# A stored shift for each attention step, applied to the list scheduler's order

## The chip, the cores and the metric

One core of one Trainium2 chip. The metric is device time in microseconds (us) of one execution. The engines are TensorE (PE; its weight loads are PEld), VectorE (DVE), ScalarE (ACT), GpSimd (POOL) and SyncE (SP, which issues most transfers). Each has its own instruction stream.

## The reference

Attention with heads mixed before and after the softmax (4 batches, 12 heads, 448 rows, 64 columns), then a SoLU layer with a layer norm (1792 tokens, 768 to 1024 to 768).

```python
scores = scale * np.matmul(q, k.transpose(0, 1, 3, 2))
scores = np.einsum('bhij,hg->bgij', scores, w_pre)
attn = softmax(scores)                       # max, exp, sum
attn = np.einsum('bhij,hg->bgij', attn, w_post)
x = np.matmul(attn, v)                       # -> (B*S, H*D)
...
h = x @ w_in
solu = h * softmax(h)
ln = (solu - mu) / np.sqrt(var + 1e-06) * g_ln
out = ln @ w_out
```

## The kernel before

Two stages run one after the other, each written as tasks (`add`, key first) that a list scheduler, `Plan.order`, puts into one list. The list is then walked and each task emits its instructions. So what the list sets is the order of the instructions within each engine's stream and nothing else: two neighbours of the list on different engines start when their inputs are there. An engine works its own stream in that order, and an instruction that waits holds up all that stands behind it on that engine.

The attention has 2629 tasks. A batch has four blocks of rows (three of 120 rows, one of 88); a block is cut into units of ten rows, taken in pairs. The tasks of a pair and their lines:

- `qk` (PE, L559): scores of two heads into two PSUM banks; `sh` (ACT, L571) writes the float16 upper half, `sl` (DVE, L576) the remainder and frees the bank. Six `qk` fill a block.
- `f` (SP): a transfer that brings ten rows of all heads together. `m` (PE, L629): the mix over heads, one step for a pair of units.
- `mx` (DVE, L639): row maximum of a unit; `ex` (ACT, L655): its exponentials and their sum; `gd`, `iv` (DVE, L666 and L670): guard and reciprocal for the pair; `w` (POOL, L676): the second mix's weights divided by the sum; `o` (PE, L684): the second mix, transposed; `po` (ACT, L284): its copy out of PSUM, which frees one of two banks.
- `av` (PE, L733): times v, six steps a block; `xh` (ACT), `xl` (DVE): the result as two float16 halves.

Beside it run tasks of the next batch: loads `ld`, maxima `am`, scale chains `sc` (one small PE step each, L247, tile `spread_...`), and the split of q and k, `hi` (POOL, L277) and `lo` (DVE L280, or POOL L473 and L474). In the last batch the input weights of the second stage are converted (`wi`), measured (`wm`) and split (`wh`, `wl`), and the first tile's `h0` products (PE, L905) are slipped in. `warm` tasks are small PE products without a use for the result; `ident` (POOL) makes the identity that they and the `tp` steps at the start need.

The order comes from `Plan.order`: at each turn, the engine that can start earliest takes, among what is ready within a short look ahead, the task with the lowest due time. Due times are written by hand and moved for each kind by `AIM`; costs are fixed numbers for each task; `LAG` adds to the landing time of a kind's transfers; `TURN` is a charge where PE changes between kinds of product; `behind` makes one task stand after another in the list.

```python
for _, e, _, run in plan.order():
    run(e)
```

The second stage (`moe`, its own plan) multiplies tile after tile by the input weights (PE, L905), normalises on DVE, ACT and POOL, and multiplies by the output weights (PE, L1528).

Of the kernel before, what the change touches and what calls it, by code (L numbers as in the profile page):

```python
# [18 lines left out]
class Plan:  # L19
# [15 lines left out]
    }  # L35
    LAG = {
        "fw": 10, "ld": 4.24, "t": 3, "xd": 7.9,
    }

    def __init__(self, **rings):  # L40
        self.size = rings
# [31 lines left out]
    def order(self):  # L73
        done, out = {}, []
# [31 lines left out]
        while len(out) < len(tasks):  # L106
            best = None
            for e, t0 in free.items():
# [21 lines left out]
            _, _, e, k, t = best  # L130
            run, on, _, _, ring, slots, dma = tasks[k][:7]
# [19 lines left out]
                    avail.add(n)  # L151
            out.append((t, e, k, run))
        return out


@with_exitstack
def kernel(
# [45 lines left out]
    NXG = NPAIR // XG  # L203
# [111 lines left out]
    plan = Plan(raw=2, hl=2, v=NV, S=2, s=2, sr=AHEAD, m=3, o=2, e=NE, w=NWR, p=RING, x=1, X=1)  # L315
# [598 lines left out]
    def add_tasks():  # L914
# [49 lines left out]
        for b in range(B):  # L964
# [4 lines left out]
            for n in "kq":  # L969
# [4 lines left out]
                for i in range(pieces):  # L974
# [5 lines left out]
                        behind=[("ld", n, b, i - 1)] if i else [("ld", "k", 0, pieces - 1)] if z and n == "q" else [],  # L980
# [145 lines left out]
            for u in range(NU):  # L1126
# [85 lines left out]
            for blk in range(NBLK[b]):  # L1212
# [18 lines left out]
                for g in range(NXG):  # L1231
                    due = av_at[XG * g + XG - 1] + 1.1
                    add(
                        ("xh", b, blk, g),
                        one(x_hi, b, blk, g),
                        {"act": (0.45, 0.57)},
                        after=[("av", b, blk, XG * (g + 1) - 1)] + ready,
                        due=due,
                        ring="X" if blk == g == 0 else None,
                        until=[("xd", b, i) for i in range(XP)],  # L1240
                    )
                    add(
                        ("xl", b, blk, g),
                        one(x_lo, b, blk, g),
                        {"dve": (0.75, 0.84)},
                        after=[("xh", b, blk, g)],
                        due=due + 0.7,
                    )
# [71 lines left out]
    with tc.manual_schedule():  # L1320
# [11 lines left out]
        add("clear", lambda e: [nc.vector.memset(t, 0.0) for t in ams.values()], {"dve": 0.5}, due=-1.0)  # L1332
        nc.vector.memset(bias64, -8.0 * (1023 - 127 + 20) * 2.0**20)
        add_tasks()
        for _, e, _, run in plan.order():
            run(e)
        st.close()

# [383 lines left out]
```

## Time and profile before

| | us |
|---|---|
| median of three runs (687.9 to 694.23) | 691.94 |
| the profiled execution | 690.71 |
| its span, first to last instruction | 689.0 |
| PE busy | 643.7 |
| DVE busy | 498.0 |
| ACT busy | 455.3 |
| POOL busy | 276.7 |

The attention's PE work ends a little after 460 us, where that of the second stage follows at once. A row of the timeline gives the start, the length, the engine and line, what it writes and reads, how many instructions are merged, and in brackets the idle time before them and what ended it. The ends of PE's products are modelled and run past the start of the next; so the time that PE spends on a step is read here from its start to the start of the next one. PEclk is the granted clock as a share of full speed (2.4 GHz); 0.50 is 1.2 GHz.

### The profile page before, as it was taken

The numbers are of one execution on the slowest core, as the hardware profiler recorded it, in microseconds if no ns is written. First come the engines' busy times: TensorE is split into PE (matmuls) and PEld (weight loads), VectorE is DVE, ScalarE is ACT, GpSimd is POOL, SyncE is SP. The second block draws the span as 40 slices with busy tenths as digits, with TensorE's granted clock in tenths as the row PEclk, the third lists the DMA queues.
The fourth block names the chain that finished last, engine by engine and source line by source line (L and its number), as shares of the span: only waits on it lengthen the run. The fifth ranks groups of instructions, "written<-read, shape, count | busy, mean of one in ns | idle before, by whom it ended". The sixth has DMA issues, their size and how long they took to land. (4 is left out here: it accounts for less than half of the span.)

```text
span 689.0 us, 17773 instructions
## 1 busy us (share of the span) xinstructions
PE 643.7 (93%) x6660; PEld 431.5 (63%) x6660; DVE 498.0 (72%) x1322; ACT 455.3 (66%) x989; POOL 276.7 (40%) x427
## 2 busy tenths in 40 slices
PE   6878999999889999899899988899999989999997
PEld 6545667777666777667677666775444435666664
DVE  5978997789978689987879999946888998200000
ACT  3867978998779988887888987552456666411111
POOL 2223871247741337851214323611667746410000
PEclk9989999999999999999989999999999999999999
DMA  9157458467777566978336843107956532451121
GB/s 237 29 146 228 158 134 190 158 181 205 214 143 143 130 191 189 244 197 235 128 113 209 272 147 95 27 2 218 225 145 142 104 61 54 89 126 46 47 64 52
DMA packets 114030, 98.54 MB, mean 143 GB/s; under 512 B 69604, under 2 KB 104600, under 8 KB 113944
## 3 DMA queue, kind: packets, MB, share of 16 engines
q1 hardware_dynamic: 108120, 83.62, 45.9%
q0 software_dynamic: 4416, 12.40, 6.5%
q10 hardware_dynamic: 1408, 1.38, 0.7%
q8 instruction: 53, 0.87, 0.5%
q14 instruction: 33, 0.27, 0.1%
HBM read 33.24 MB, written 9.63 MB: 62 GB/s over the span
## 5 line engine op out<-in xcount | busy, mean ns | idle before, releaser
L684 PE MATMUL po<-wr,e 128*112 128x120 f32 x1440 | 184.1, 278 | 14.1 <-POOL wr L676 12.2
L684 PEld LDWEIGHTS po<-wr,e 128*112 128x112 f32 x1440 | 161.3, 181 | 53.4 <-POOL wr L676 27.4
L676 POOL TENSOR_SCALAR wr<-wq,sm 128x120 f32<-128x120 f32 x180 | 69.2, 393 | 211.0 <-DVE sm L670 117.4
L655 ACT ACTIVATE e<-pm,nb,c_exp 128x448 f32<-128x448 f32 x180 | 131.7, 733 | 26.3 <-DVE dead L639 24.0
L639 DVE TENSOR_SCALAR_CACHE_REDUCE dead<-pm,c_nexp 128x448 f16<-128x448 f32 x180 | 121.6, 676 | 15.9 <-PE pm L629 9.2
L284 ACT COPY p_t<-po 112x480 f32<-112x480 f32 x180 | 109.5, 618 | 28.3 <-PE po L684 26.9
L576 DVE SCALAR_TENSOR_TENSOR s<-ps,s 120x448 f16<-120x448 f32 (+1 forms) x192 | 112.3, 616 | 16.3 <-ACT s L571 15.2
L571 ACT ACTIVATE s<-ps 120x448 f16<-120x448 f32 (+1 forms) x192 | 93.8, 545 | 18.9 <-PE ps L559 16.9
L733 PE MATMUL px<-p_t,raw_v 112*64 112x120 f32 (+3 forms) x1632 | 88.0, 259 | 2.0 <-ACT e L655 0.8
L905 PE MATMUL ps_h<-wi,xf 128*128 128x512 f16 x396 | 86.1, 379 | 2.6 <-DVE u L1455 2.6
L559 PE MATMUL ps<-k,q 64*64 64x448 f16 (+2 forms) x1008 | 81.8, 362 | 6.5 <-DVE s L576 5.1
L733 PEld LDWEIGHTS px<-p_t,raw_v 112*64 112x64 f32 x1632 | 76.0, 137 | 15.3 <-issue 9.1
L1528 PE MATMUL y<-wo_h,lth 128*128 128x384 f16 (+2 forms) x224 | 73.0, 326 | 0.0
L1528 PE MATMUL y<-wo_l,lth 128*128 128x384 f16 (+2 forms) x224 | 73.0, 326 | 0.0
L1528 PE MATMUL y<-wo_h,ltl 128*128 128x384 f16 (+2 forms) x224 | 73.0, 326 | 0.0
L905 PEld LDWEIGHTS <-xf 128*128 128x128 f16 x396 | 38.7, 98 | 49.3 <-issue 3.1
L1540 ACT ACTIVATE o<-y,c_out 128x384 f32<-128x384 f32 (+2 forms) x28 | 16.2, 579 | 72.6 <-PE y L1528 72.6
L629 PE MATMUL pm<-sr,wp_hi 64*64 64x448 f16 x720 | 59.1, 366 | 5.2 <-DMA sr<-s 3.2
L1528 PEld LDWEIGHTS <-lth 128*128 128x128 f16 x448 | 43.8, 98 | 29.3
L559 PEld LDWEIGHTS <-q 64*64 64x64 f16 (+2 forms) x1008 | 32.8, 107 | 33.6 <-issue 16.2
L1513 POOL TENSOR_TENSOR ll<-u,lh 128x1024 f16<-128x1024 f32 x14 | 31.6, 2258 | 16.7 <-ACT lh L1509 10.8
L666 DVE TENSOR_SCALAR sm<-sm 128x2 f32<-128x2 f32 (+1 forms) x92 | 25.2, 275 | 17.7 <-ACT e L655 16.9
(182 smaller groups left out, 823.4 us busy)
## 6 DMA issues: line engine op xcount, KB each, us to landing
sr<-s SPq DMA_DIRECT2D x176, 210.0 KB
cv_wi<-in_moe_w_in_dram SPq DMA_DIRECT2D x24, 256.0 KB
cv_wo<-in_moe_w_out_dram SPq DMA_DIRECT2D x8, 768.0 KB
raw_k<-in_k_dram POOLq DMA_DIRECT2D x18, 224.0 KB, 4.3
raw_q<-in_q_dram POOLq DMA_DIRECT2D x18, 224.0 KB, 6.2
raw_v<-in_v_dram POOLq DMA_DIRECT2D x18, 224.0 KB, 4.8
xh<-xsh SPq DMA_DIRECT2D x9, 224.0 KB
xl<-xsl SPq DMA_DIRECT2D x9, 224.0 KB
```

The lines of the kernel that those rows point to most:

```text
L284: nc.scalar.copy(out=out, in_=in_)
L559: nc.tensor.matmul(sps[b, c, h + e][lo:hi], q2[b, g][rows, 2 * j + x, i0 + lo : i0 + hi], k1[b, g][rows, 2 * j + y], start=(a == 0), stop= ...
L571: nc.scalar.activation(out=s_t[b, c][0 : y.shape[0], h, 0], in_=y, func=AF.Copy, scale=2.0**-E_S)
L576: nc.vector.scalar_tensor_tensor(out=t[:, h, 1], in0=y, scalar=2.0**-E_S, in1=t[:, h, 0], op0=ALU.mult, op1=ALU.subtract)
L629: nc.tensor.matmul(pmx[b, u + i][64 * e : 64 * e + 64, 0:S], w[rows], sr[b, u][rows, e, z], start=(a == 0), stop=(a == 2),)
L639: nc.vector.tensor_scalar(out=dead, in0=pmx[b, u][:, 0:S], scalar1=c_nexp[0:UK, b : b + 1], scalar2=None, op0=ALU.mult, op1=ALU.min, accum ...
L655: nc.scalar.activation(out=ee[b, u], in_=pmx.pop((b, u))[:, 0:S], func=AF.Exp, bias=nbs.pop((b, u)), scale=c_exp[0:UK, b : b + 1], accum_o ...
L676: ENG[eng].tensor_scalar(out=w, in0=wq[0:UK, 0 : H * UN], scalar1=sm, scalar2=1.0, op0=ALU.mult, op1=ALU.mult)
L684: nc.tensor.matmul(ps[:, c * 120 : (c + 1) * 120], e[:, c * CP : (c + 1) * CP], w, start=True, stop=True)
L733: nc.tensor.matmul(xps[b, blk, g][e * 64 : e * 64 + 64, i, cut], raws["v", b, p][:, e, c * D : (c + 1) * D], next(x for y, x in block_view ...
L905: nc.tensor.matmul(ps[:, n], xx[:, kc, o : o + 128], ww[:, kc, n * 512 : (n + 1) * 512], start=(kc == 0 and a == 0), stop=(kc == KDM - 1 a ...
L1528: nc.tensor.matmul(ys[t, n], lts[t, x][:, kc], w[:, kc, c0:c1], start=(kc == 0 and a == 0), stop=(kc == KFF - 1 and a == 2),)
```

## The change

`Plan` gets a list of 2629 whole numbers, `SHIFT`, and a function that applies it: the task at place i of the new list is the one that stood at place i plus the i-th number. Three inputs of the scheduler change too: `LAG` has 1 us more for the transfers `f`; the second `ex` of a pair stands behind the first in the scheduler's list; and `xh` steps stand behind each other in order. The tasks themselves, their buffers, the engines they run on and the second stage's plan are as they were.

```diff
     LAG = {
-        "fw": 10, "ld": 4.24, "t": 3, "xd": 7.9,
+        "f": 1, "fw": 10, "ld": 4.24, "t": 3, "xd": 7.9,
     }
+
+    SHIFT = """
+    2 2 3 3 3 3 6 7 1 -8 0x2 -12 -9 15 20 16 20 21 21 88 7 -4 1 113 102 32 30 -15 -3 75 17 -9 -13 -13 15
+    -9 16 22 -14 -25 14 23 68 -28 17 63 111 -18 -18 -16 -10 -16 -15 -12 -12 -12 -11 -11 -10 -27 -16 -10
...
+    1 1 1 1 1 2 -51 -1 0x11
+    """
...
+    def shifted(self, out):
+
+        moves = []
+        for x in self.SHIFT.split():
+            a, _, n = x.partition("x")
+            moves += [int(a)] * int(n or 1)
+        return [out[i + a] for i, a in enumerate(moves)]
...
                     one(expo, *g),
                     {"act": (0.701, 0.816)},
                     after=[("mx",) + g],
+                    behind=[("ex", b, u0)] if u != u0 else [],
...
                         one(x_hi, b, blk, g),
                         {"act": (0.45, 0.57)},
                         after=[("av", b, blk, XG * (g + 1) - 1)] + ready,
+                        behind=[("xh", b, blk, g - 1)] if g else [("xh", b, blk - 1, NXG - 1)] if blk else [],
...
-        for _, e, _, run in plan.order():
+        for _, e, _, run in plan.shifted(plan.order()):
             run(e)
```

## Rows read from the trace of the kernel before

**Rows 1.** Busy time by stretch: stretch, its length, engines, clock, DMA share, GB/s
```profile
60.00:460.00 400.00, 376.56 (x4760) 280.19 (x4760) 345.60 (x953) 330.05 (x763) 183.12 (x331) 0.98 0.60 165
460.00:560.00 100.00, 96.93 (x615) 46.74 (x614) 81.31 (x173) 48.98 (x77) 55.00 (x35) 1.00 0.61 149
560.00:689.00 129.00, 124.78 (x744) 72.61 (x742) 26.54 (x69) 37.26 (x59) 23.29 (x16) 1.00 0.28 68
```
**Rows 2.** PE's timeline in a stretch without gaps
```profile
130.66 0.57 PE L629 MATMUL pm<-sr,wp_hi 64*64 64x448 f16 x8
...
131.25 0.74 PE L559 MATMUL ps<-k,q 64*64 64x448 f16 x12
131.92 1.07 PE L684 MATMUL po<-wr,e 128*112 128x120 f32 x8
132.93 1.04 PE L733 MATMUL px<-p_t,raw_v 112*64 112x120 f32 x16
...
136.13 1.90 PE L684 MATMUL po<-wr,e 128*112 128x120 f32 x16
137.95 0.76 PE L559 MATMUL ps<-k,q 64*64 64x448 f16 x12
...
142.78 0.57 PE L629 MATMUL pm<-sr,wp_hi 64*64 64x448 f16 x8
...
143.47 1.07 PE L684 MATMUL po<-wr,e 128*112 128x120 f32 x8
```
**Rows 3.** Groups by line, 60 to 440 us: busy us, mean ns, idle before, releasers
```profile
L684 PE MATMUL po<-wr,e 128*112 128x120 f32 x1327 | 168.8, 277 | 10.9 <-POOL wr L676 9.1 <-ACT p_t L284 1.1 <-issue 0.2
...
L655 ACT ACTIVATE e<-pm,nb,c_exp 128x448 f32<-128x448 f32 x165 | 120.8, 733 | 22.4 <-DVE dead L639 20.2 <-DVE sm L666 1.6
...
L284 ACT COPY p_t<-po 112x480 f32<-112x480 f32 x166 | 101.0, 619 | 21.2 <-PE po L684 19.7
...
L277 POOL TENSOR_SCALAR hl_q<-raw_q,p_q 112x512 f16<-112x512 f32 x18 | 13.3, 760 | 0.9 <-DVE p_q L232 0.7
```
**Rows 4.** PE's timeline, four of its nine longest gaps, first and last among them
```profile
183.15 1.89 PE L684 MATMUL po<-wr,e 128*112 128x120 f32 x16 [1.58 <-POOL wr L676]
...
285.69 3.45 PE L684 MATMUL po<-wr,e 128*112 128x120 f32 x16 [2.19 <-POOL wr L676]
...
342.18 0.75 PE L559 MATMUL ps<-k,q 64*64 64x448 f16 x10 [1.47 <-DVE s L576]
...
446.11 3.45 PE L684 MATMUL po<-wr,e 128*112 128x120 f32 x16 [2.01 <-POOL wr L676]
```
**Rows 5.** DVE's timeline ahead of the last of these gaps
```profile
439.16 6.05 DVE L280 SCALAR_TENSOR_TENSOR wi<-wi,p_wi,wi 128x1024 f16<-128x1024 f32 x3
445.14 0.16 DVE L666 TENSOR_SCALAR sm<-sm 128x2 f32<-128x2 f32 x1
```
**Rows 6.** ACT's timeline ahead of the first of these gaps
```profile
178.50 0.72 ACT L655 ACTIVATE e<-pm,nb,c_exp 128x448 f32<-128x448 f32 x1
...
179.21 0.61 ACT L284 COPY p_t<-po 112x480 f32<-112x480 f32 x1
179.69 0.74 ACT L655 ACTIVATE e<-pm,nb,c_exp 128x448 f32<-128x448 f32 x1
```
**Rows 7.** Busy time at half clock, three of four stretches, first and last among them, as rows 1
```profile
41.00:46.00 5.00, 4.24 (x44) 1.70 (x35) 3.71 (x11) 2.62 (x7) 0.78 (x3) 0.50 0.53 139
...
344.00:350.00 6.00, 6.00 (x40) 3.92 (x32) 4.42 (x11) 3.81 (x9) 0.00 (x0) 0.50 0.48 163
446.00:449.00 3.00, 2.89 (x14) 2.89 (x15) 3.00 (x4) 0.61 (x1) 0.40 (x2) 0.50 0.00 0
```
**Rows 8.** PE's timeline, its first products
```profile
5.77 3.38 PE L539 MATMUL warm<-ident 128*128 128x128 f16 x30 [5.77 <-POOL ident masks.py:199]
```
**Rows 9.** Line 280 on DVE: durations in ns (least, median, most), first and last start
```profile
L280 DVE SCALAR_TENSOR_TENSOR hl_k<-raw_k,p_k,hl_k x20: 466/724/909, 90.7 to 289.3; 112x256 f16<-112x256 f32 x20
L280 DVE SCALAR_TENSOR_TENSOR hl_q<-raw_q,p_q,hl_q x18: 467/480/946, 96.3 to 299.2; 112x256 f16<-112x256 f32 x18
```

More of the change, by code (lines that the diff above doesn't have):

```diff
@@ L36 @@
     LAG = {
-        "fw": 10, "ld": 4.24, "t": 3, "xd": 7.9,
+        "f": 1, "fw": 10, "ld": 4.24, "t": 3, "xd": 7.9,
     }
+    SHIFT = """
+    2 2 3 3 3 3 6 7 1 -8 0x2 -12 -9 15 20 16 20 21 21 88 7 -4 1 113 102 32 30 -15 -3 75 17 -9 -13 -13 15
+    -9 16 22 -14 -25 14 23 68 -28 17 63 111 -18 -18 -16 -10 -16 -15 -12 -12 -12 -11 -11 -10 -27 -16 -10
+    -7 0 3 4 -8 -5 2 5 7 0 -12 -20 -9 -2 0 1 2 -13 -8 -13 0x4 2 -1 -9 0 1 -16 -11 1 6 -8 -4 0 11 -9 2 4
[8 rows of a table added]
+    1 8 0 2 -4 -2 4 -1 5 -15 -11 -7 -4 18 -3 -3 0 4 -3 0 -3 -1 4 0 3 8 4 -3 -6 -4 -2 1 6 -4 0x4 1 -25
@@ new lines @@
+    0x2 2 -1 4 0 5 8 5 9 4 -1 -6 -1 6 6 16 0 4 6 -17 -14 5 1 -8 -2 4 4 7 10 -4 6 -4 9 4 -2 7 3 -29 5 -4
+    4 10 4 -3 1 12 13 1 2 3 -3 3 8 14 2 6 7 1 16 5 24 4 0 3 -11 4 7 9 14 8 9 7 -4 8 16 -5 15 -5 8 9 5 8
+    16 -8 -4 15 10 14 15 4 15 1 3 13 22 14 11 14 14 0 8 21 12 20 25 13 11 12 18 4 10 13 16 24 21 0 14 10
+    -35 -32 -26 -17 -94 -90 -75 -107 -71 -30 -57 -27 1 -6 0x2 4 -1 5 -1 9 5 -1 4 14 8 17 1 -4 3 4 -9 4
+    -8 -3 5 -6 4 -1 7 2 8 5 5 8 5 7 7 -4 7 11 7 -1 12 5 12 13 3 5 14 17 3 4 -71 6 6 -63 -32 -23 -30 -15
@@ new lines @@
+    -14 -10 2 -6 1 6 -5 -4 10 11 0 -2 9 2 2 8 8 -4 -4 10 12 1 4 -15 3 -13 -7 -20 0 1 -5 3 -1 2 5 10 -3
+    0x2 -3 0 3 8 8 3 -3 -5 2 -2 -1 -7 1 1 1 1 2 0 1 3 0 2 -1 2 2 4 4 0x2 2 -6 3 0 3 -1 2 -1 1 -60 1 1 3
+    3 -4 5 5 7 0 3 -3 4 6 0 -5 4 1 -1 -14 1 3 0 3 -1 0 2 2 2 5 9 4 5 -6 -3 -3 2 6 -5 -3 1 1 9 1 1 7 1 1
+    2 5 -4 4 8 -4 3 3 -3 8 9 0 4 0 4 -23 -2 -61 -3 -11 5 0x2 4 -4 4 -2 7 4 7 -4 8 5 -3 -3 -2 4 -9 6 2 6
+    -18 1 -8 1 2 2 2 3 -11 0 2 2 2 6 9 -4 -1 -16 2 2 2 5 -6 -6 1 2 -8 -3 1 7 0 2 -4 2 8 -4 -4 -3 -1 1 5
@@ new lines @@
+    7 -3 3 3 4 8 -4 -10 -8 3 -1 -8 -2 -2 0x3 2 2 8 1 5 9 10 4 -2 9 -10 -10 20 2 3 4 6 7 -11 1 -8 -13 -17
[12 rows of a table added]
+    4 -3 0 2 -1 2 2 2 -2 1 -10 2 2 -1 2 -4 -1 1 2 0 4 1 3 0 5 1 2 9 13 -2 -13 1 3 -12 -3 -1 13 0x3 -7 1
+    -12 2 6 14 1 4 5 11 -10 3 4 -7 -11 8 1 -13 3 8 -8 -3 0 -15 2 3 4 -12 -4 3 7 -6 -3 8 -1 0 11 -1 1 11
+    -9 10 -8 5 1 -5 7 15 1 3 -6 7 -14 7 2 9 -14 -14 8 -5 -5 -4 -3 -17 -3 2 2 -4 -3 0 6 0 -2 0 16 0 6 -5
+    -4 -2 13 -2 1 13 -4 0x2 1 -4 8 -3 3 3 -2 -5 7 11 21 7 -21 -19 -2 1 -2 8 4 -6 -3 3 -17 -4 -3 3 11 -1
[13 rows of a table added]
@@ new lines @@
+    -54 -40 -37 -30 -26 -7 -2 -20 -19 30 1 7 1 -12 0x2 -4 -1 27 2 3 -4 -3 -1 2 -5 -2 17 0 18 0 3 0 3 3
+    -8 -11 1 18 11 13 -8 -2 0 -9 4 6 -1 7 5 8 13 8 15 18 6 3 5 7 -17 9 9 -221 3 9 12 -72 -57 -27 -21 -19
+    -14 -5 -2 0 1 -13 -2 1 4 7 7 -4 6 0x2 5 11 8 8 35 -9 8 -7 7 -14 -1 13 8 -6 -20 -9 -3 4 37 6 -2 -5 6
[14 rows of a table added]
+    -44 -1 0 1 -8 -7 -5 -1 1 -2 0 4 4 -2 -2 -1 3 0x2 2 4 1 3 0 -11 8 0 -7 9 -2 -2 -1 0 -4 -3 7 15 2 5 9
+    15 -5 -8 -5 10 -1 10 10 10 -8 9 21 22 -18 -14 5 -11 5 -6 -6 1 3 3 12 2 15 3 -20 10 10 13 -3 -1 0 -28
@@ L40, in __init__ @@
+    -25 8 9 7 14 9 9 -33 4 -8 -3 2 5 11 6 1 3 -15 3 6 9 1 1 -31 7 7 -20 -39 -2 -1 3 -1 3 -6 0 1 2 0 1 1
+    1 1 1 1 1 2 -51 -1 0x11
+    """
     def __init__(self, **rings):
```

47 rows, old and new, of the table SHIFT are left out of this document.

## The prediction

> **What bounds the kernel now.** I read the busy time by stretch first [rows 1]. From 460 us on PE is busy for 96.9 of 100 us and then 124.8 of 129: the second stage is PE's work end to end, its tasks are untouched, so it starts earlier or later with the attention and stays as long. All that the change can move lies ahead of 460 us. Between 60 and 460 us PE is busy 376.6 of 400 us, DVE 345.6, ACT 330.1, POOL 183.1. So PE is nearest to its limit and idles 23.4 us; a reader should see that DVE and ACT have 54 and 70 us left, which is not much.
>
> Then PE's timeline in a stretch without gaps [rows 2]. There the steps follow each other start to start, and their sum is the elapsed time: in such a stretch no order of the other engines helps, only fewer or cheaper PE steps. But the price of a step depends on its neighbours. One `o` takes 132.93 - 131.92 = 1.01 us, two in a row take 137.95 - 136.13 = 1.82, so a second of its kind saves 0.20. An `m` takes 0.59 ahead of a `qk` (131.25 - 130.66) and 0.69 ahead of an `o` (143.47 - 142.78), so joining these saves 0.10. A change of kind on PE thus costs 0.10 to 0.20 us.
>
> Last I listed every gap of PE from 60 to 460 us and read what ended it. Some thirty gaps make 22.1 us; the nine of 1 us and more hold 13.6 of it: 1.58, 1.43, 1.10, 2.19, 1.47, 1.31, 1.45, 1.06 and 2.01 us, from 183.15 to 446.11 [rows 4]. Most end with POOL's `w`: the groups by line put 9.1 of the 10.9 us ahead of `o` on it [rows 3]. `w` itself is short; late is the chain `mx`, `ex`, `ex`, `gd`, `iv`, `w`. Two places show why. Ahead of 446.11, DVE runs three `wl` steps, 6.05 us, and the guard that PE needs starts at 445.14, right behind them [rows 5]. Ahead of 183.15, ACT puts a copy `po` between the two `ex` of the pair, 0.61 us [rows 6].
>
> After some of these gaps the clock is at 0.50, 1.2 GHz of 2.4. The first of four such stretches is 41 to 46 us, behind short gaps while the first units' transfers land; the others follow the gaps at 281 to 286, 340 to 344 and 444 to 446. PE is busy in them for 4.2, 3.0, 6.0 and 2.9 us [rows 7], 16.1 in all, and half of that, 8.0 us, is lost: the `o` pair at 446.11 takes 3.45 us instead of 1.9 [rows 2, 4].
>
> **The change part by part.** Nothing is added or removed; every step keeps its work. `LAG` and the two `behind` entries touch the planner's list alone and put no wait on the chip. I laid the 2629 shifts on the order that the planner of the kernel before gives, also 2629 tasks. It fits but for three tasks at places 202 to 210, which then stand ahead of what they need, so names are sure to a place or two there and elsewhere as good as exact. Of the places within an engine's stream, which alone count, PE keeps the task in 230 of 558, DVE in 128 of 781, ACT in 186 of 640, POOL in 100 of 308, SP in 151 of 254. So this is no small edit, even if most moves go past a few tasks.
>
> *Kinds on PE.* From the first `o` on and without `warm`, PE's tasks change their kind of tile (as the planner's `TURN` counts it) 294 times before and 260 times after. The `o` steps stand in 95 runs instead of 106, `av` in 50 instead of 56, and `m` with `qk` beside it 54 times instead of 45. At 0.10 to 0.20 each [rows 2] 34 changes are 3.4 to 6.8 us. I take -5.0; the stretches where PE waits anyway are 6% [rows 1].
>
> *The gaps.* I looked up each of the nine. Five lose what ended them. At 446.11 the guard stands ahead of the `wl` steps (2.01). At 342.18 two `wi` steps of DVE go behind the `sl` that PE waits for (1.47). At 195.07 a `lo` step goes behind the guard (1.10). For two of the scale products, `spread_v` (1.43, 1.45), the maxima stand earlier on ACT or PE has other steps ahead of it. The other four (1.58, 2.19, 1.31, 1.06) change in part: at 183.15 one of two `lo` steps and the copy leave, but PE also comes 0.97 us earlier; at 285.69 both `lo` steps stay and an `av` comes between. Whole for 7.5 us and half for 6.1 us gives -10.5.
>
> The same shows over all pairs. The two `ex` of a pair stand side by side on ACT 40 times out of 88 instead of 11; 49 copies lie between them instead of 89, at 0.62 us each [rows 3]. Long DVE steps (`lo`, `wi`, `wl`, `am`) between the last row maximum and the guard fall from 66 to 43. PE has less than 5 us of own work between `m` and its `o` in 11 cases instead of 19.
>
> Against that, an order that packs PE tighter must make new gaps, and some moves point there: `w` stands right behind a load, `hi`, `lo` or the like on POOL 68 times instead of 56, at up to 0.76 us [rows 3], so up to 9 us of lateness, which PE's work between `m` and `o` covers in most pairs. SP's transfers move past each other too (transposes behind fetches); no gap of PE after 60 us was ended by a transfer, so I give this nothing; if that cover went, a late fetch would hold `m`, as it does near 40 us. I take 4 us of new gaps, between 0 and the whole 10.5, nearer to the rows for POOL halved. Net -6.5.
>
> *The clock.* Two of the four half clock stretches stand behind gaps that go (340 to 344, 444 to 446). They cost 3.0 and 1.4 us. Into the first, at 40 us, eleven `warm` steps move between the products that wait there, so PE has something to do; half of its 2.1 us would be 1.0. The third, at 286, stays. I take -4.5, between 0 and -8.0 [rows 7].
>
> *The start.* PE's first product waits until 5.77 us for the identity [rows 8], which POOL makes behind the masks; in the new order it comes first, and 28 `warm` steps instead of 15 precede the first transpose. The scale chains behind them wait for loads that are not moved. I take -1, between 0 and -3.
>
> Sum: -5.0 - 6.5 - 4.5 - 1.0 = -17.0. From the profiled execution's 690.7 that is 673.7; the median of the runs shown lies 1.2 above it, so **675 us**.
>
> A rule that speaks against it: the planner has fixed costs, but a `lo` step on DVE was seen at 467 to 946 ns, the same shape [rows 9]. The Trainium skill, page "SBUF — State Buffer", section "SBUF: two separate sides", says that a DVE operation with two SBUF inputs and a GpSimd operation that reads SBUF hold a shared port pair exclusively, the other waiting in full. By that rule a new order that puts `lo` beside POOL's `hi` and `w` pays on both; the spread of the row agrees. As a mechanism it is part of rival 1, and I give it 0.05 of that chance.
>
> **The rivals.**
> 1. *The gain is swallowed.* The gaps only move: other `w`, or `lo` and `hi` steps that now run beside each other, are late instead. If all 20 of the medium `hl_q` and `hl_k` cases went to their longest, 18 x 0.47 + 20 x 0.19 = 12 us of DVE time would be added [rows 9], against 54 us free. For it: DVE and ACT are at 86% and 83% in this stage [rows 1], and a tighter PE has less slack. Against: the enders of the long gaps leave by name. Then the kinds (-3.4) and a part of the clock (-2) stay: 685 to 687.
> 2. *Slower: the copies come late.* Forty copies leave their place between two `ex` and run behind the second. A copy frees one of two banks, so the `o` after next waits. If each cost PE the 0.71 us of one `ex` (179.21 - 178.50 in [rows 6]) that were 28 us, and 675 becomes 703. It decides from 24 of the 40 on (24 x 0.71 = 17), and is over 1% slower from 34 on. Against: in the kernel before ACT waits 19.7 us for `o` and PE only 1.1 us for copies [rows 3], so copies run early and have room.
> 3. *All of it goes.* No gap (-23.4), no half clock (-8.0), -6.8 for kinds, -3 at the start: 650. Against: DVE would be at 93% of a stage of 370 us (345.6 / 370), with chains across four engines.
>
> **How the numbers follow.** A measurement of this kernel tells about 1% from no change. Forecast (664 to 684) 0.66; rival 1 (684 to 699) 0.19; rival 2 (over 699) 0.09; rival 3 (below 664) 0.06. The forecast's own ends are its terms' bounds: all at their best -10.5 - 6.8 - 8.0 - 3.0 = -28, 664 on the runs' footing; kinds at their least with a third of the rest 684. Faster by over 1% (below 685.0) 0.73, slower by over 1% (above 698.9) 0.09, within 1% 0.18. The range 662 to 692 leaves out rival 2, most of rival 3 and the upper end of rival 1, 0.2.
>
> **What would show it.** Right: PE idle from 60 to 460 us falls from 23.4 us to some 17 for the same work; `o` waits less for `w` than 9.1 us; no gaps at the places of 342 and 446 us; `o` runs of two at 1.82; the second stage as long as before. The clock term is wrong if half clock stretches still hold 16 us of PE's time; the kinds' term if PE's busy time in the attention does not fall by about 5 us beyond what the clock gives. The forecast is wrong if PE waits for `p_t` copies by many us (rival 2), or if DVE's `lo` group grows over its 0.72 and 0.48 us medians and new gaps of the old size stand elsewhere (rival 1).

## The result

The changed kernel takes **667.37 us** (median of four runs, 665.76 to 669.91), the kernel before 691.58 beside it: a ratio of 0.966, 95% interval 0.960 to 0.971. The forecast was 675 in a range of 662 to 692. The direction, the range and the place were right, but the time lies 7.6 us under the forecast. The profiled execution of after has 665.8 us and a span of 663.4, 25.6 under that of before.

### The profile page after: what moved, and what is told of

It reads as the page before. It is cut to its first block, busy times and chain, and to the rows that moved or that the text cites. A ratio compares the mean times of both kernels' runs of the same rounds, so it can differ in the third digit from the quotient of the medians.

```text
span 663.4 us, 17760 instructions
## 1 busy us (share of the span) xinstructions
PE 633.8 (96%) x6660; PEld 432.4 (65%) x6660; DVE 480.8 (72%) x1322; ACT 451.8 (68%) x989; POOL 280.4 (42%) x427
## 5 line engine op out<-in xcount | busy, mean ns | idle before, releaser
L768 PE MATMUL po<-wr,e 128*112 128x120 f32 x1440 | 176.6, 274 | 6.2 <-POOL wr L760 4.5
L768 PEld LDWEIGHTS po<-wr,e 128*112 128x112 f32 x1440 | 157.3, 178 | 36.7 <-POOL wr L760 16.0
L760 POOL TENSOR_SCALAR wr<-wq,sm 128x120 f32<-128x120 f32 x180 | 77.2, 437 | 192.8 <-DVE sm L754 89.8
L739 ACT ACTIVATE e<-pm,nb,c_exp 128x448 f32<-128x448 f32 x180 | 131.7, 736 | 20.5 <-DVE dead L723 9.1
L368 ACT COPY p_t<-po 112x480 f32<-112x480 f32 x180 | 108.3, 625 | 10.8 <-PE po L768 9.6
L655 ACT ACTIVATE s<-ps 120x448 f16<-120x448 f32 (+1 forms) x192 | 97.5, 554 | 25.3 <-PE ps L643 19.9
L817 PE MATMUL px<-p_t,raw_v 112*64 112x120 f32 (+3 forms) x1632 | 86.6, 259 | 1.0 <-ACT e L739 0.7
L643 PE MATMUL ps<-k,q 64*64 64x448 f16 (+2 forms) x1008 | 80.2, 360 | 5.5 <-DMA q<-hl_q 2.5
L713 PE MATMUL pm<-sr,wp_hi 64*64 64x448 f16 x720 | 58.2, 363 | 4.5 <-DMA sr<-s 3.2
L643 PEld LDWEIGHTS <-q 64*64 64x64 f16 (+2 forms) x1008 | 34.4, 107 | 28.9 <-issue 8.7
L739 ACT ACTIVATION_READ_ACCUMULATOR e<-pm,nb,c_exp 128x1 f32 x180 | 38.1, 211 | 0.0
```

Of the source, the lines that this page charges most:

```text
L368: nc.scalar.copy(out=out, in_=in_)
L643: nc.tensor.matmul(sps[b, c, h + e][lo:hi], q2[b, g][rows, 2 * j + x, i0 + lo : i0 + hi], k1[b, g][rows, 2 * j + y], start=(a == 0), stop= ...
L655: nc.scalar.activation(out=s_t[b, c][0 : y.shape[0], h, 0], in_=y, func=AF.Copy, scale=2.0**-E_S)
L713: nc.tensor.matmul(pmx[b, u + i][64 * e : 64 * e + 64, 0:S], w[rows], sr[b, u][rows, e, z], start=(a == 0), stop=(a == 2),)
L739: nc.scalar.activation(out=ee[b, u], in_=pmx.pop((b, u))[:, 0:S], func=AF.Exp, bias=nbs.pop((b, u)), scale=c_exp[0:UK, b : b + 1], accum_o ...
L760: ENG[eng].tensor_scalar(out=w, in0=wq[0:UK, 0 : H * UN], scalar1=sm, scalar2=1.0, op0=ALU.mult, op1=ALU.mult)
```

## The profile after

Line numbers of after are 84 to 86 higher: `o` is L768, `w` L760, `ex` L739, `m` L713, `qk` L643, `po` L368, the guard L750. First the busy time by stretch, with the columns of [rows 1]; the attention now ends near 435 us.

```profile
60.00:435.00 375.00, 363.99 (x4774) 279.13 (x4773) 330.10 (x958) 327.84 (x768) 188.97 (x334) 1.00 0.64 176
435.00:535.00 100.00, 97.00 (x613) 46.64 (x612) 82.71 (x177) 49.39 (x79) 55.55 (x35) 1.00 0.65 150
535.00:663.00 128.00, 124.14 (x742) 72.20 (x739) 26.18 (x66) 36.61 (x57) 22.65 (x16) 1.00 0.28 68
```

The last two lines stand for the second stage and are as in [rows 1]: all of the gain lies in the attention. There PE idles 375.00 - 363.99 = 11.0 us instead of 23.4, and no half clock is left behind 60 us. POOL's 189 us against 183 is a longer busy time in a shorter stretch.

Where in the attention? I cut it at a step that both kernels reach at nearly the same time, the first `o` steps of batch 2: before at 261.6 us, after at 260. The same view, first before, then after:

```profile
60.00:261.60 201.60, 193.87 (x2483) 142.51 (x2483) 173.36 (x504) 170.63 (x400) 98.75 (x192) 1.00 0.66 172
261.60:460.00 198.40, 182.70 (x2279) 137.67 (x2279) 172.24 (x452) 159.41 (x363) 84.37 (x140) 0.97 0.54 157
```
```profile
60.00:260.00 200.00, 192.49 (x2497) 144.34 (x2496) 171.96 (x509) 171.65 (x405) 99.48 (x193) 1.00 0.68 173
260.00:435.00 175.00, 171.50 (x2279) 134.79 (x2279) 158.13 (x451) 156.19 (x364) 89.50 (x141) 1.00 0.60 179
```

In the first halves PE idles 7.7 and 7.5 us, the same. In the second it is 15.7 against 3.5, and DVE is busy for 158.1 us with the steps that took it 172.2. Seen from the step's own times, `o(2,6)` ends 1.9 us earlier and the last `o` of the attention 25.6 us earlier. So half of the new order brings next to nothing and the other half brings nearly all, and DVE's own steps have become shorter there.

The groups by line answer to [rows 3] (busy us, mean ns, idle before, releasers). [rows 3] stop at 440 us, ahead of the last long gap, so here is its first row again for 60 to 460 us; then after, 60 to 435 us:

```profile
L684 PE MATMUL po<-wr,e 128*112 128x120 f32 x1382 | 176.8, 278 | 12.9 <-POOL wr L676 11.1 <-ACT p_t L284 1.1 <-issue 0.2
```
```profile
L768 PE MATMUL po<-wr,e 128*112 128x120 f32 x1394 | 169.4, 273 | 5.9 <-POOL wr L760 4.2 <-ACT e L739 0.9 <-ACT p_t L368 0.3
...
L739 ACT ACTIVATE e<-pm,nb,c_exp 128x448 f32<-128x448 f32 x172 | 125.9, 737 | 19.0 <-DVE dead L723 9.1 <-DVE sm L750 4.2 <-DVE sm L754 2.2
L368 ACT COPY p_t<-po 112x480 f32<-112x480 f32 x171 | 103.5, 628 | 10.2 <-PE po L768 9.0 <-PE px L817 0.8
```

PE's wait for `w` ahead of `o` falls from 11.1 to 4.2 us, that for `p_t` copies from 1.1 to 0.3. `ex` waits 9.1 us for its row maxima (`dead`) instead of 21.7.

PE's timeline has four gaps of 0.95 us and more after the first `o`; these three hold 5.7 us, and the fourth is 0.95 at 413.37:

```profile
51.71 0.58 PE L713 MATMUL pm<-sr,wp_hi 64*64 64x448 f16 x1 [2.00 <-DMA sr<-s]
53.45 0.90 PE L713 MATMUL pm<-sr,wp_hi 64*64 64x448 f16 x3 [1.16 <-DMA sr<-s]
...
220.15 0.77 PE L643 MATMUL ps<-k,q 64*88 64x448 f16 x6 [2.53 <-DMA q<-hl_q]
```

All nine long gaps of [rows 4] are gone or under a microsecond. The first two lines here are at the start, where before had 1.42 us ahead of the same `m.0.8`; the third is new, and a transfer ended it.

Busy time at half clock, to be held against [rows 7]:

```profile
34.63:41.46 6.83, 6.83 (x57) 3.82 (x57) 3.60 (x12) 2.90 (x9) 0.00 (x0) 0.50 0.56 148
51.70:58.53 6.83, 5.66 (x30) 3.94 (x34) 2.75 (x9) 3.31 (x8) 0.42 (x2) 0.50 0.67 191
```

Apart from one in the last microseconds, which both kernels have, these are all. The three late ones of before are gone, but the start has two instead of one.

The 25.6 us of the spans, split by first `o`, last `h0` and PE's busy time between them (worked out from the two traces; "full clock work" is busy time less what half clock cost):

| us | before | after | difference |
|---|---|---|---|
| first `o` starts at | 45.97 | 43.84 | -2.1 |
| PE idle, first `o` to last `h0` | 26.1 | 14.3 | -11.8 |
| lost to half clock there | 6.8 | 2.8 | -4.0 |
| PE's full clock work there | 391.4 | 383.8 | -7.6 |
| from the last `h0` to the end | 218.7 | 218.6 | -0.1 |

## Experiments

Two readings stand against each other. *By causes*: the gain is the sum of the edits that the prediction named (exponentials side by side, guards ahead of long DVE steps, kinds joined), each of which can be had alone. *By the whole*: the order pays only where the streams of all five engines fit each other. All kernels do the whole computation. They differ in the stored shifts alone; the diffs name steps in one engine's stream, which says more than the numbers of the shifts.

### One edit alone, put into the old order

`b_exps`: on ACT, the copies between the two `ex` of a pair go behind the second wherever dependences allow, 89 such copies become 4 (the new order has 49).

```diff
 ex 0 2
+ex 0 3
 po 0 0
-ex 0 3
 po 0 1
```

> The kernel before with ACT's stream alone edited: wherever a copy po stands between the two exponentials of a pair it goes behind the second, so copies between the two fall from 89 to 4 (the changed kernel has 49). Theory A (each shorter chain pays by itself): PE's 9.1 us of waiting for w between 60 and 440 us fall by about half and one of the clock's dips goes: -4 to -7 us, 685 to 688. Theory B (the gain is in the joint order; one rule alone only moves the wait): within 2 us of the kernel before. Rival 2 of the prediction (late copies cost PE up to 0.71 us each): 88 copies, up to +60 us; any slowing of over 5 us with PE waiting for p_t speaks for it.

Measured: 693.29 us, ratio 1.002 (0.999 to 1.006). No gain at all. The place of [rows 6] shows why. ACT's, then DVE's, then PE's timeline of `b_exps`:

```profile
180.93 0.72 ACT L676 ACTIVATE e<-pm,nb,c_exp 128x448 f32<-128x448 f32 x1
...
181.63 0.72 ACT L676 ACTIVATE e<-pm,nb,c_exp 128x448 f32<-128x448 f32 x1
```
```profile
181.48 2.84 DVE L301 SCALAR_TENSOR_TENSOR hl_k<-raw_k,p_k,hl_k 112x256 f16<-112x256 f32 x4
184.24 0.15 DVE L687 TENSOR_SCALAR sm<-sm 128x2 f32<-128x2 f32 x1
```
```profile
185.58 1.59 PE L705 MATMUL po<-wr,e 128*112 128x120 f32 x13 [1.58 <-POOL wr L697]
```

The copy is gone from between the two, the second `ex` ends by 182.35, and the guard still starts at 184.24, because DVE is in its `lo` steps until then. PE's gap stays 1.58 us, to the hundredth. Two causes stood there in a row. The prediction named both for this gap, but its price for all pairs, 0.62 us for each copy, is that of the one that did not bind.

Elsewhere the edit did move something. The list of waits (engine, line and what it waited for; us in total, times, longest) has for PE in `b_exps`:

```profile
PE po L705 <- POOL wr L697: 10.0, 11, 2.2
...
PE po L705 <- ACT p_t L305: 2.9, 4, 1.9
```

Before, these are 12.2 and 1.1 us. The list puts some of the new gaps down to other steps, but ten gaps of 0.35 us and more ahead of `o`, 6.9 us in all, end 0.10 to 0.14 us behind the copy that frees the bank which this `o` needs; in before there are two such gaps, 2.4 us. So where copies were moved back they came late, as rival 2 of the prediction had it, and took again what the shorter wait for `w` gave.

`b_guards`: on DVE, guards and reciprocals go ahead of the long steps `lo`, `wi`, `wl`, `am` that stand between the last row maximum and the guard (66 such steps become 18; the new order has 43).

```diff
 mx 0 8
-am k 1 0
 gd 0 6
 iv 0 6
-am k 1 1
 gd 0 8
 iv 0 8
+am k 1 0
+am k 1 1
```

> The kernel before with VectorE's stream alone edited: a lo, wi, wl or am step that stands between a pair's last row maximum and its guard goes behind the reciprocal, where the order allows it: 66 such steps fall to 18 (the changed kernel has 43). Theory A: the gaps at 183, 195, 285 and 446 us lose most of their 6.9 us and the half clock behind two of them goes (3.2 us): -6 to -9 us, 683 to 686. Theory B: the steps put back delay what they feed, -2 to +2 us.

Measured: 709.26 us, ratio 1.026 (1.022 to 1.031), slower. From the list of waits, DVE's guard before and in `b_guards`, then PE's main waits in `b_guards`:

```profile
DVE sm L666 <- ACT e L655: 16.9, 23, 1.7
```
```profile
DVE sm L683 <- ACT e L672: 28.6, 36, 1.8
```
```profile
PE po L701 <- POOL wr L693: 10.1, 15, 2.2
PE ps L576 <- DVE s L593: 8.6, 21, 1.6
PE pm L646 <- ACT e L672: 8.5, 9, 1.5
```

The guard brought forward arrives before the exponentials it needs, and DVE stands still in front of it 11.7 us longer. The row maxima behind it come late (the exponentials wait for them 41.1 us instead of 24.0), and PE's wait moves from `o` (12.2 us before) to `m` and `qk` (1.6 and 5.1 us before). The long step ahead of the guard was partly useful filling.

`b_both` has the two edits together.

> Both edits on the kernel before, PE's, POOL's and SP's streams untouched. Theory A: the two add up to -9 to -14 us, more than half of the 24 us of the change, without any change of kinds on PE. Theory B: at most -4 us, since PE's own order is still the old one.

Measured: 706.26 us, ratio 1.024 (1.019 to 1.029). The pairing does not rescue the guards.

`b_merge`: on PE, 16 single `o` steps wait for the next `o`; 294 changes of kind become 267.

```diff
 qk 0 3 0
+m 0 17
 o 0 12
-m 0 17
 o 0 13
```

> The kernel before with 16 o steps of PE put behind the one m, qk or av step that stood between them and the next o: 267 changes of kind instead of 294, all other streams as they were. At 0.23 us a change: -6 us, 684 to 687, if the gaps stay at 26 us. If the delayed o steps make copies and the next weights late, the gaps take it back: 690 or more.

Measured: 701.10 us, ratio 1.015 (1.011 to 1.018), slower in spite of 27 fewer changes. PE's waits:

```profile
PE ps L573 <- DVE s L590: 7.5, 21, 1.7
...
PE pm L643 <- ACT e L669: 4.8, 10, 0.9
```

An `m` or `qk` that comes one step earlier is earlier than what it needs (`e` frees the `pm` bank, `s` the `ps` bank), 7.5 and 4.8 us instead of 5.1 and 1.6.

None of the edits that the prediction named gave any of the gain when put alone into the old order. `b_exps` and `b_guards` go further than the new order does (4 copies against its 49, 18 long steps against its 43); the new order's own part of these moves was not tried alone.

### The streams of one order with those of the other

`pe_new` has PE's stream from the new order; the other engines keep the old one as far as dependences permit (DVE differs in 50 of 781 places, ACT in 135 of 640, POOL in 54 of 308). `pe_old` is the mirror image.

```diff
 pe_new, from the kernel before
-PE: before's order
+PE: after's order (328 of 558 places differ)
 pe_old, from the kernel after
-PE: after's order
+PE: before's order (328 of 558 places differ)
```

> PE's stream is the changed kernel's to the step (260 changes of kind); the other engines' streams are the kernel before's but for what PE's order forces (61 pairs of VectorE's steps stand the other way round, where the change has 1402; ScalarE 165 of 610, GpSimd 31 of 345, SyncE none of 150). Theory A (PE's order brings the cheaper kinds, the other streams bring the shorter gaps, and the two add up): 34 fewer changes at 0.23 us each as a_split priced them, -8 us, PE's idle time from the first o to the last h0 about 26 us as before: 682 to 686. Theory B (the orders only work together): PE waits for producers that come in the old order, idle time well over 26 us, 688 or more.

> The reverse: PE's stream is the kernel before's (294 changes of kind), the other streams are the changed kernel's as far as PE's order lets them be (VectorE differs from it in 160 pairs of 1402, ScalarE in 92 of 610, GpSimd in 8, SyncE in 9). Theory A: the gaps shrink from 26 to about 14 us and most of the half clock goes: -12 to -16 us, 676 to 680. Theory B: no gain, 688 or more.

Measured: 776.08 (ratio 1.122, 1.117 to 1.126) and 763.22 (1.104, 1.098 to 1.110). PE's waits in `pe_new`, then in `pe_old`:

```profile
PE pm L667 <- ACT e L693: 24.6, 23, 3.8
PE po L722 <- POOL wr L714: 24.5, 19, 4.3
PE ps L597 <- DVE s L614: 22.2, 28, 3.5
```
```profile
PE po L765 <- POOL wr L757: 20.5, 14, 3.4
```

In both, PE idles more than 66 us between the first `o` and the last `h0`, and half clock costs 28 to 32 us there. Either PE order is good with its partners and bad with the other's: PE waits for what the others make or free (`e`, `w`, `s`). The streams of the other four engines were not exchanged one by one.

### The price of a change of kind

`a_split` takes the new order and puts 46 `o` steps behind the PE step that followed them: 260 changes become 337.

```diff
 o 0 1
+m 0 6
 o 0 2
-m 0 6
 qk 0 2 0
```

> The changed kernel with 46 of its o steps each put behind the next PE step of another kind (m, qk or av): PE changes its kind of tile 337 times instead of 260, nothing else moves on PE, other streams are the same. If a change of kind costs the 0.10 to 0.20 us that the timeline of the kernel before showed: +8 to +15 us. If the price is only seen where PE waits anyway: under +3 us.

Measured: 690.58 us, as slow as before (ratio 0.999, 0.996 to 1.002) and 23.2 us over after. That is 0.30 per change, but not all of it is the change itself. PE's waits show a part of the rest:

```profile
PE pm L711 <- ACT e L737: 7.6, 17, 1.0
PE ps L641 <- DVE s L658: 5.4, 18, 0.9
```

Against 1.2 and 2.1 us in after. For the price proper I took, from the traces, the medians from a step's start to the next one's, without a gap between them and at full clock (a dash where there are fewer than three cases):

```
previous, step, next         before   after   a_split
qk  o  o   (first of two)     0.911   0.911   0.911
    o  m   (second of two)    0.913   0.913   0.913
    o  m   (last of three)    0.975   0.975     -
qk  o  m   (alone)            1.004     -     1.004
o   m  qk                     0.592   0.592   0.592
o   m  o                      0.692     -     0.692
av  av av  (120 rows)         0.820   0.820
av  alone  (120 rows)         0.971   0.971
```

An `o` alone costs 0.093 us more than one beside another, an `m` or `qk` ahead of an `o` about 0.10 more than one ahead of its like, and a run of `av` 0.15 more for its two ends. Counted over the streams, the new order has 25 instead of 51 lone `o` steps, 64 instead of 85 entries from `m` or `qk` into `o` and 50 instead of 56 runs of `av`: 26 x 0.093 + 21 x 0.10 + 6 x 0.15 = 5.4 us. For `a_split` (105 lone, 105 entries, 53 runs) it is 80 x 0.093 + 41 x 0.10 + 3 x 0.15 = 12.0 of the 23.2. Of the other half, the profile shows 5.2 us as longer idle time of PE between the first `o` and the last `h0`, and 1.7 in the second stage, which was not edited; the rest stays open. For `b_merge` the table gives a gain of 3.7 us, and the run a loss of 10.2.

The last of three `o` is not dearer by kind. In 16 of the 17 runs of three in before, and 12 of the 14 in after, the third `o` starts 0.11 to 0.14 us behind the end of the copy that frees the first one's bank. The step ahead of it then takes about 0.96 and it 0.975, together 0.11 more than without a wait: in the two runs where the copy was done earlier and nothing else was late they take 0.911 and 0.912 or 0.913. The modelled ends of the products cover this wait, and the list of gaps does not show it.

### The gain by stretch

`half_early` has the new order for the first 1475 of the 2629 planned tasks and the old one behind; `half_late` the reverse. Up to four tasks lie on the other side of the cut, so all engines change over together.

```diff
 half_early, from the kernel before, all engines
-before's first 1475 tasks
+after's first 1475 tasks
 the rest in before's order
 half_late, from the kernel before, all engines
 before's first 1475 tasks
-the rest in before's order
+the rest in after's order
```

> The new order for the first 1475 of the 2629 planned tasks (to the first o steps of batch 2, about 260 us), the old order for the rest; 1 to 4 tasks stand on the other side of the cut, so all engines change over at the same place. In the two profiled executions the new kernel is only 1.3 to 1.9 us ahead at o(2,5) and o(2,6), and 7 of the 34 fewer changes of kind lie here (287 instead of 294). Theory A (an order pays by stretch: what a stretch gains stays gained, and nothing before it is needed): 688 to 691, within 1% of the 691.6 before. Theory B (the order gains only as one whole, its second half needs what the first half prepares, and the other way round): a seam of two orders costs like a mixture of streams, over 695.

> The old order for the first 1475 tasks, the new order from there; 267 changes of kind. Theory A: the 24 us that the new kernel gains behind o(2,6) come here as well, 691.6 - 24 = 667 to 670, with gaps of the old size up to 260 us and small ones behind it. Theory B: 675 or more, since batch 2's and 3's transposed operands and loads come from the old half's order; with over 691 the gain would be gone.

Measured: `half_early` 691.67 (ratio 1.001, 0.998 to 1.004), `half_late` 670.02 (0.971, 0.968 to 0.975). Busy time by stretch, `half_early`, then `half_late`:

```profile
60.00:258.50 198.50, 190.33 (x2465) 143.69 (x2464) 169.77 (x501) 168.83 (x398) 99.90 (x194) 0.99 0.69 174
258.50:455.00 196.50, 180.90 (x2283) 135.37 (x2282) 172.04 (x452) 159.44 (x365) 84.07 (x140) 0.98 0.55 158
```
```profile
60.00:261.50 201.50, 194.42 (x2484) 142.95 (x2485) 173.00 (x502) 170.47 (x401) 97.40 (x190) 1.00 0.67 172
261.50:436.50 175.00, 171.08 (x2281) 134.94 (x2280) 158.58 (x451) 155.97 (x364) 89.59 (x141) 1.00 0.61 179
```

PE's idle time of the second stretch goes with the order: 15.6 us where the old order runs, 3.9 where the new one runs, as in the kernels that they come from (15.7 and 3.5). So both readings had a part. In these runs the order could not be taken apart by engine or by edit, but by time it could: 175 us of new order for all engines give 20 of the 24 us, with the old order ahead of them.

### The pairing in the new order

`a_unpair`: in 20 of the 40 pairs whose `ex` stand side by side, a copy goes back between them.

```diff
 ex 0 4
+po 0 1
 ex 0 5
-po 0 1
 po 0 2
```

> The new order with one edit on ACT's stream: in 20 of the 40 pairs whose two ex stand side by side a copy po goes back between them (49 copies between become 69; before had 89). Theory 1, the pairing is one of the causes of the gain (the prediction's reading): each puts 0.62 us on the second ex, and where PE is packed tight part of it reaches PE: 4 to 12 us slower than the new kernel's 667.4, so 671 to 679. Theory 2, the pairing is beside the point, as it was in the old order, where pairing nearly all of them brought nothing: within 2 us of 667.4.

Measured: 672.97 us, ratio 0.975 (0.972 to 0.979), 5.6 over after by the medians, inside the range of Theory 1. But the trace, 6.8 us longer, lets only a part of it stand against the edit. The first `o` starts 1.7 us later already; on the way there PE's first scale product of `q` waits 3.8 instead of 1.9 us. By `o(0,8)` the delay is 2.7 us; two of the twenty pairs lie on that way, and PE's waits for transfers, and which of them did it stays open. From there to 407 us of after the delay stays between 2.7 and 3.3 us, past sixteen of the pairs. Then it grows by 1.6 us at one gap and by 0.5 right behind it, at the scale step of `wi`. The stage from the last `h0` on is 1.6 us longer, where nothing was edited: the clock is at half from 539.29 to 542.70 us, which after does not have. PE's timeline at the one gap, after, then `a_unpair`:

```profile
413.37 1.07 PE L768 MATMUL po<-wr,e 128*112 128x120 f32 x8 [0.95 <-ACT e L739]
```
```profile
418.10 1.07 PE L766 MATMUL po<-wr,e 128*112 128x120 f32 x8 [2.54 <-POOL wr L758]
```

The copy makes the second `ex` end 0.6 us later, against PE, and with it the guard. But the gap grew by 1.59. DVE's timeline at this guard, then POOL's, first after, then `a_unpair`:

```profile
410.37 0.25 DVE L750 TENSOR_SCALAR sm<-sm 128x2 f32<-128x2 f32 x1 [0.34 <-ACT e L739]
```
```profile
410.57 2.40 POOL L922 TENSOR_TENSOR wi<-cv_wi 128x1024 f32<-128x1024 f32 x1
```
```profile
414.15 2.13 DVE L748 TENSOR_SCALAR sm<-sm 128x2 f32<-128x2 f32 x1 [0.84 <-ACT e L737]
```
```profile
413.85 2.41 POOL L920 TENSOR_TENSOR wi<-cv_wi 128x1024 f32<-128x1024 f32 x1
```

In after the guard starts 0.20 us ahead of POOL's product and takes 0.25 us. In `a_unpair` it starts 0.30 us behind its start, takes 2.13, and ends (416.28) as the product does (416.26). It was held. So Theory 2 is right for sixteen of the twenty pairs, and at the one that counts, most of the price was not the copy but a step of POOL that the guard then met. That made me look for such guards in the old order.

### Guards that meet POOL's product

In before, four of the attention's guards take 1.7 to 2.3 us instead of 0.17, at 339.34, 365.72, 398.18 and 418.23; each ends with the product of `wi` on POOL that started ahead of it. In after the longest guard is 0.82. The first of the four, DVE's timeline, then POOL's:

```profile
339.34 2.07 DVE L666 TENSOR_SCALAR sm<-sm 128x2 f32<-128x2 f32 x1
```
```profile
338.97 2.41 POOL L838 TENSOR_TENSOR wi<-cv_wi 128x1024 f32<-128x1024 f32 x1 [3.15 <-DVE cv_wi L835]
341.80 0.71 POOL L676 TENSOR_SCALAR wr<-wq,sm 128x120 f32<-128x120 f32 x2 [0.42 <-DVE sm L670]
```

PE's gaps at 342.18, 372.15, 401.18 and 425.16, four of the nine, stand 0.8 to 4.7 us behind the ends of these guards. `b_port` puts these four products behind the two `w` steps that the guard feeds (POOL's stream, no other changes; names as in the planner, the last number of `wi` is the product).

```diff
-wi 0 5
 w 2 41
 w 2 42
+wi 0 5
```

> The old order with four steps of POOL's stream moved, and nothing else: the products of wi (a POOL product of 128x1024, 2.41 us each) that start just ahead of a DVE guard go behind the two w steps that this guard feeds. In the profiled execution of before these four guards (128x2, 0.17 us as a rule) take 2.07, 1.73, 2.00 and 2.28 us and end within 0.05 us of POOL's product beside them (339.34, 365.72, 398.18, 418.23); in the new kernel no guard in the attention takes longer than 0.83. Theory P (the held guards are a cause of the gaps behind them): the guards take 0.17 again, 7.4 us of DVE's time come free, the gaps at 342.18 (1.47), 372.15 (1.31), 401.18 (1.45) and 425.16 (1.06) shrink or go, 4 to 5 us, and with the first of them perhaps the half clock behind it (3.4): 682 to 687. Theory W (only the order as a whole counts, another chain is as late at each of these places, as in the single edits so far): the guards are short, the gaps stay, 689 to 693; slower if the products, now later, meet other guards.

Measured: 688.24 us (twelve runs) beside 689.88, ratio 0.997 (0.994 to 0.9995): between the two expectations, 0.05 to 0.6% faster, and the only single edit of the old order that made it faster at all. The same two views of `b_port`:

```profile
338.70 0.16 DVE L678 TENSOR_SCALAR sm<-sm 128x2 f32<-128x2 f32 x1
```
```profile
339.92 2.41 POOL L850 TENSOR_TENSOR wi<-cv_wi 128x1024 f32<-128x1024 f32 x1
```

Three of the four guards are short now; for the second, the moved product met the next guard instead (1.93 us at 362.61). The gaps of 1.31 and of 1.47 are gone (0.51 us is left near the latter), 1.06 became 0.92, and the one ahead of the scale product of `v` (1.45) went to a later `qk`, 1.26; a new one of 0.64 stands at 367.19. PE's idle time between the first `o` and the last `h0` is 22.2 instead of 26.1 us; 0.9 of that lies at `m.0.8` at the start, where nothing was edited, and 2.8 behind `o(2,6)`. So what stood at these four places is a cause of gaps, but of about 3 us of the 11.8 in the profile, and of about 2 in the runs.

Two things go with this edit, and it does not separate them. The product holds DVE's guard, and it also stands ahead of the `w` steps in POOL's own stream. Behind the first product POOL waits only 0.42 us for the reciprocal, so `w` would not have been much earlier without the hold. What loses the whole 2 us by the hold are DVE's next steps: the `s` that PE waits for at 342.18 starts at 341.52, and the maxima for the scale product of `v` at 400.88, each less than 0.8 us behind its guard's end.

The hold itself repeats. In the traces of all fourteen kernels 25 guards start 0.15 to 1.00 us behind the start of such a product, and all of them end 0.02 to 0.03 us behind its end; five start 0.20 us ahead of it and take 0.25 or 0.26 us.

### The gaps that the new order made

`a_fix` goes at the two gaps of after. `m.0.8` moves behind two `o` and a `qk` step. The last `hi` and `lo` steps of batch 2's `q` move ahead of `w` and DVE steps that they had been put behind, and on SP the last transposes of `k` and `q` go ahead of two fetches `f` each (POOL's stream, in part):

```diff
 hi q 2 3
+hi q 2 4
+hi q 2 5
 w 1 25
 w 1 24
-hi q 2 4
...
 w 1 28
-hi q 2 5
```

> The changed kernel with two places mended. At the start the step m of unit 8 goes behind o.0.3, o.0.4 and a qk, since it waits 2.00 and 1.16 us there for its transfers, and the 6.8 us at half clock behind that wait cost 2.8 us. In batch 2, the last hi and lo steps of q go some places earlier on GpSimd and VectorE and two transposes two fetches earlier on SyncE, since a qk waits 2.53 us for the last transpose at 220 us. If these waits are PE's own loss: -4 to -8 us, 659 to 663. If the next chain is as late as this one: within 2 us of the changed kernel.

Measured: 664.21 us, ratio 0.961 (0.957 to 0.964); after has 0.966 (0.960 to 0.971), so the times alone do not tell them apart. The trace does: both gaps are gone (at the start 0.82 us ahead of `m.0.6` and 0.83 ahead of a `qk` stand in their place), PE idles 10.6 instead of 14.3 us from the first `o` to the last `h0`, and the last `o` of the attention ends 5.4 us earlier. Some 1.5 us are lost again in the second stage, which was not edited: there PE waits 2.33 us at one place in both kernels, and in `a_fix` half clock follows. Busy time at half clock in that stage:

```profile
528.55:531.97 3.42, 3.09 (x8) 1.13 (x8) 2.94 (x12) 1.80 (x4) 1.69 (x1) 0.50 0.55 107
```

## Why the prediction was right, and where it was not

**What bounds the kernel** held: PE in the attention, with the second stage as long as before (218.7 and 218.6 us). PE is busy for 364 of 375 us now.

**Kinds, -5.0 forecast.** By the price table it is -5.4; [rows 2] gave the prices rightly. PE's full clock work fell by 7.6. Of the 2.2 beyond, some 0.4 are four fewer runs of three `o` that wait for a copy, 0.11 us each, mostly unseen because the modelled end of the product before covers them. The other 1.8 stay open. `b_merge` says that such covered waits can be as large as the kinds: it has fewer changes and 3.8 us more full clock work, with the same `m` and `qk` steps taking 3.5 and 1.5 us longer. The Trainium skill, page "TensorEngine Tiling (Array Packing)", section "Key Properties", says that going from one tiling mode to another drains TensorE. The 0.05 to 0.10 us at each boundary agree with it.

**The gaps, -6.5 forecast, -11.8 measured.** This is the term that was mis-sized. I took the nine long gaps as five gone and four halved. In the trace the five are gone, and of the other four 1.58 became 0.64, 2.19 became 0.51, and the 1.31 and 1.06 vanished: 12.5 us instead of 10.5. The 4 us of new gaps were about right in size: the new ones of 0.5 us and more after 60 us are 0.76, 0.91, 2.53 and 0.95, in all 5.2. What is missing in the sum are the shorter gaps. From 60 us on they held 9.8 of the 23.4 us of idle time, and I put their change at nothing without a reason. Of the seven between 0.5 and 1 us (4.6 in all) one is left, 0.70, and what lies in gaps under 0.5 us fell from 5.3 to 4.0: 5.1 us together, the largest part of the miss.

The cause of the largest new gap was not the one named, `w` behind loads on POOL. It is SP's queue. SP's timeline of after, then DVE's:

```profile
209.78 1.70 SPq L694 DMA_DIRECT2D sr<-s  x2
211.59 4.33 SPq L570 DMA_TRANSPOSE q<-hl_q  x1
216.36 4.66 SPq L694 DMA_DIRECT2D sr<-s  x4
```
```profile
206.37 1.38 DVE L364 SCALAR_TENSOR_TENSOR hl_q<-raw_q,p_q,hl_q 112x256 f16<-112x256 f32 x2
```

PE waits at 220.15 for a transposition of `q`. The last `lo` step ahead of it ends at 207.75, and SP issues it only at 211.59, behind a transposition of `k` and two fetches; in the old order it stands right behind that of `k`. "I give this nothing" was wrong here: I argued from the absence of such gaps in the old order, in which those steps stood elsewhere. `a_fix` shows that the 2.53 us were a matter of order alone; it moved the `hi`, `lo` and SP's steps together and does not tell them apart.

**The reasons for the gaps** were named too simply. I read for each gap the step that ended last and took its removal as the gain. `b_exps` and `b_guards` had more pairing and fewer long steps ahead of guards than the new order, and brought no gain and +18 us. A gap ends with the last of several chains; to take away one shows nothing if the next is as late (1.58 us in `b_exps`, to the hundredth), and the step taken away has to stand somewhere, where it makes another chain late. And ahead of four of the nine gaps, two of which I had put down to `wi` steps and to maxima, a guard of 0.17 us had been held for 2 by POOL. The row at 339.34 with 2.07 us for 128x2 elements was in the trace of before; I looked at what stood ahead of guards, not at how long they took themselves.

**The clock, -4.5 forecast.** From the first `o` on it is -4.0. The forecast counted the first stretch too, which lies mostly ahead of that: from the start to the last microseconds, half clock cost 9.4 us before (not 8.0; the windows of [rows 7] cut its stretches short) and 6.3 after, -3.1. So the term was near by luck, since its parts were others. All three late stretches went, also the one at 286 that I had staying, behind a gap that shrank from 2.19 to 0.51: 6.5 us. In exchange the eleven `warm` steps did not spare the start its stretch, and a second came behind `m.0.8`, 2.8 us.

**The start, -1 forecast.** The first product waits 1.42 us for the identity instead of the 5.77 in [rows 8], and the first `o` starts 2.1 us earlier. But `o(0,8)` ends at 63.47 instead of 62.41: the gain was given back within 20 us, to the transfers of `m.0.8` and the half clock behind them.

**The rivals.** Rival 1 falls in the main: new gaps came, but less than a third of the old. Its mechanism on the port I had the wrong way round. I held it to be what a new order might lose; it is what the old order lost. The four guards alone cost DVE 7.4 us more than their 0.17 each, about half of the 14.1 us by which its busy time fell behind 260 us. The Trainium skill, page "SBUF — State Buffer", section "SBUF: two separate sides", says that some DVE operations and a GpSimd operation lock a shared pair of ports for the whole instruction, and the other waits in full. The guards agree: the first ends at 339.34 + 2.07 = 341.41, POOL's product beside it at 338.97 + 2.41 = 341.38. Line 280's `lo` steps, on which I had weighed the rule, show no sum either way:

```profile
L364 DVE SCALAR_TENSOR_TENSOR hl_k<-raw_k,p_k,hl_k x20: 472/574/908, 88.2 to 284.7; 112x256 f16<-112x256 f32 x20
L364 DVE SCALAR_TENSOR_TENSOR hl_q<-raw_q,p_q,hl_q x18: 459/635/977, 95.4 to 298.6; 112x256 f16<-112x256 f32 x18
```

By the medians that is 20 x 0.574 + 18 x 0.635 = 22.9 us against 23.1 in [rows 9]. Rival 2 did not come: in the gaps PE waits 0.3 us for copies, and some 1.3 us unseen in runs of three `o`. But what it describes exists, as the ten gaps of `b_exps` show. Rival 3 came nearer than I gave it: the idle time from 260 us on is nearly all gone (3.5 of 175 us), but from 60 to 260 us nothing went.

**What stays open.** By the runs about 20 of the 24 us lie behind 260 us, by the profiles 23.7 of 25.6: 12.2 of idle time, 6.5 of half clock and 4.9 of full clock work. Of the work 3 to 4 are kinds (by the table, for `half_late`), and of the idle time about 3 go with the products that held guards. For the other 9 us of gaps I can say where they were but not put them down to single edits, and why the half clock went with them is not shown either.

## To carry to other kernels

Compare two orders by PE's idle time and by each engine's busy time in stretches between common steps: where the same steps have become shorter, the order has taken them out of each other's way, and no list of enders shows it. Look for instructions that take many times the median of their kind before a pattern is made a rule. Count transfers and their producers among the steps moved, even if no gap of the old order ends with one.

## What the chip showed beyond that

- A guard of 128x2 elements takes 0.17 us, or up to 2.28 beside a POOL product of 2.41. In these traces the one that starts first decides: 0.15 us behind the product's start it is held to the end, 0.20 us ahead of it, it takes 0.25.
- Gaps are a property of the order. The one ahead of `o(1,18)` is 1.58 us in before, `b_exps`, `b_merge` and `half_late`, and 0.64 in after, `half_early` and `a_unpair`.
- Half clock isn't. The second stage is the same in all kernels, and some 89 us into it each of the fourteen profiles has a gap of 2.33 or 2.34 us on PE. In seven of them a stretch of 3.4 us at half clock follows, in the other seven none does; from the last `h0` to the end the seven take 220.0 to 220.6 us, the others 218.6 to 219.0. In the attention, the gap ahead of `o(2,17)` is 2.17 to 2.19 us in before, `b_exps`, `b_merge`, `b_port` and `half_early`, and half clock follows in all five; that ahead of `o(3,38)` is 2.00 or 2.01 us in the same five, and half clock follows in before alone. And behind the same gap and with the same order, `half_early` has a stretch at half clock and after has none. PE's timeline of `half_early`, and its stretch by windows, against the line at 220.15 above and 1.00 in that stretch of after:

```profile
217.49 0.76 PE L609 MATMUL ps<-k,q 64*88 64x448 f16 x6 [2.49 <-DMA q<-hl_q]
```
```profile
218.65:222.06 3.41, 3.41 (x19) 3.41 (x19) 1.15 (x2) 2.58 (x7) 0.35 (x1) 0.50 0.61 168
```

So from these traces a forecast can name gaps behind which the clock may fall, but not that it falls there, and 1 to 2 us between two kernels can be this alone.
